# A 26-product second matmul in the last two token groups, and a spread transform tail

## The chip, the cores and the metric

The kernel runs on one core of a Trainium2 chip. A core has engines that work beside each other, each with its own queue of instructions: TensorE (PE) multiplies matrices, VectorE (DVE) and ScalarE (ACT) work on tiles in on-chip memory (SBUF) and in the matmul accumulators (PSUM), GpSimd (POOL) works on SBUF, and SyncE (SP) mostly starts transfers (DMAs). An instruction that waits holds up all that stand behind it in its own queue. The metric is the device time of one execution in microseconds (us). All data is fp32.

## The reference

Attention within chunks of 64 tokens, for 8 batches, 8 heads, 576 tokens and 64 channels a head, gives x of 8 x 576 x 512. Then comes a Fourier mix with a feed-forward block:

```python
attn = softmax(q_c @ k_c^T / sqrt(64)); x = attn @ v_c      # per chunk of 64 tokens
mixed = real(fft(fft(x, axis=1), axis=2))
u = x + mixed
un = (u - mean(u)) / sqrt(var(u) + 1e-6)                     # over 512 channels
ch = maximum(un @ w1, 0) @ w2                                # 512 x 2048, 2048 x 512
return u + ch
```

## The kernel before, in words

**Groups.** The 4608 token rows are cut into nine groups of four tiles of 128 rows. Groups 0 to 7 hold most of one batch each, in pairs of a lower and an upper tile; group 8 holds the four tiles that are left over from the middle chunks. The main loop runs `mlp(g)` for the nine groups: an "up" (un @ w1, relu) and a "down" (@ w2, added to u and stored). Each is a generator of steps, and t counts the steps over the whole kernel. `begin[g]` is the step at which group g begins; KF is 16, HF is 8.

**Products.** Group 0 multiplies plainly: `up_first`, and `down_plain` (16 steps of four matmuls dn, L1236; L1249 adds u). From group 1 on, `up_halves` and `down_halves` treat the matrices as 2x2 blocks and make 7 products where 8 would be plain. The up (L1289, accumulators pa and pb) goes through w1 in four pairs of 7 products; ACT and DVE put the accumulators together (L1294 to L1309). The down (L1341) makes 7 products of two rows of eight matmuls: 112 matmuls of 128x128 by 256. Its operand sums are made during the up by `operands` (L1167 and L1168 on DVE, L1169 on POOL), its output sums by DVE (L1350 to L1361) and POOL (L1353, L1354, L1373, L1378).

The down of the last group, `down_few` (L1405), cuts the matrices in 4x4 by 4x2 blocks and makes 26 products of four matmuls, 104 in all. The list `PRODUCTS` gives for each product its operand, its weight block, its accumulator, what DVE adds to the output after it (L1415), and the operand sums that POOL makes behind it (`sums`, L1183). Six operand sums (`EARLY`) are made during the up. `FEW` is the first group whose down is done in this way.

**Weights.** In group 0 the weights arrive and are rounded by DVE and ACT (`round_weight`, L362 to L386). POOL makes the sums of w1's blocks (`keep1`, four sums for each of four pairs, L1069) and of w2's (`keep2`, L1087). They are stored in DRAM (`keep1_store`, L1091; L1099 for w2) as slabs. Group 1's up still reads the parts of w1 where they were made; later groups fetch slabs, all on SP's queue: `fetch(1)` brings w1 slabs of 256 KB into a ring of ten (tile wa, L1155), `fetch(2)` w2 slabs of 1 MB into a ring of three (tile wb, L1160), `fetch(3)` the blocks for `down_few`, 512 KB each, into a ring of NS3 places (L1158): six in wb, the rest in tiles named more.

**make_rest.** Of the blocks that `down_few` multiplies by, 19 are sums. `make_rest` computes them on POOL in two halves of the columns: for each half it loads eight blocks of w2 (L1124, 256 KB each), makes 23 sums (`MADE`, L1133) and stores 19 of them (L1140). Buffers come from a list `spare` of 14 places that attention and transform no longer use; a buffer whose sum is stored comes free when the store has landed. It is a generator, advanced in the main loop from t = `ready_at[NG - 3]` on, two sums a step, and in the kernel before it ends during group 7's down.

**Attention and transform.** `side(b)` is the attention and transform of batch b, cut into `sizes[b - 1]` steps that are spread over the feed-forward steps before group b begins. In the main loop `due` is the number of side steps that must be done by step t, from `ready_at`. The end of the transform is a list of mixes (L838, three for an odd batch), each read by ACT (L843) and DVE (L848, L849), added to x (L855 on DVE and POOL), and normalised: `normed` writes un on ACT (L992), `turned` transposes it on PE (L397, pt) and copies it (unT, L1007), `combined` makes the three block sums of the up on DVE (L1024 to L1026). For group 1 the last three are called from `down_plain` of group 0 at given steps m. The attention uses the accumulator `att` of pool ps_a for its scores (sc, L448) and DVE transposes for q and k (L416); L418 copies one column of each transposed tile on POOL.

**Stores.** `store` writes a finished tile. A lower tile goes by POOL (L1037). An upper tile goes by four transfers of 64 KB, two from SP and two from ACT (L1046).

Queues are in program order; the tile framework adds the waits on data and on free buffers, and a rotation of eight lanes for SP's transfers, so that each waits for the one eight before it.

Of the kernel before, what the change touches and what calls it, by code (L numbers as in the profile page):

```python
# [16 lines left out]
def kernel(  # L17
# [36 lines left out]
    CH = 64  # L54
# [100 lines left out]
    NR2, NS3 = len(PRODUCTS), 11  # L155
# [245 lines left out]
    def att_T(n, which="qk"):  # L401
# [4 lines left out]
        if n > first[2]:  # L406
            for src, dst, nm in ((qs, qT, "qT"), (ks, kT, "kT")):
                if nm[0] not in which:
                    continue
                a = src.pop(n).rearrange("p j (t b d) -> p j t b d", t=4, b=2)[:, :, :, 0]  # L410
                t = one_p.tile([128, NJ, 2, CH + 1], FP32, tag=nm, name=nm)
                low = kind(n) == LO and nm == "qT"
                to = t[:, :, :, CH:0:-1] if low else t[:, :, :, 0:CH]
                if kind(n) == HI:
                    to = to[:, :, ::-1]
                nc.vector.transpose(out=to.rearrange("p j c (r t) -> p j t c r", t=4), in_=a)  # L416
                if low:
                    nc.gpsimd.tensor_copy(t[:, :, :, 0:1], t[:, :, :, CH:CH + 1])  # L418
                dst[n] = t.rearrange("p j c t -> p (j c) t")
            if n + 1 < NT:  # L420
                load(n + 1, which)
            return
# [369 lines left out]
    def fourier(b):  # L792
# [36 lines left out]
        def mixed(i):  # L829
            mix = ps_t.tile([128, 512], FP32, tag="pt", name="mix")  # L830
# [142 lines left out]
    uns, unTs = {}, {}  # L973
# [56 lines left out]
    def store(n, o):  # L1030

        last = n in groups[-1][1::2]
        for h, (b, c) in enumerate(chunks(n)):
# [37 lines left out]
    def keep1_store(i):  # L1071
        pair, o = i // NO, (2, 1, 5, 3, 0, 4, 6)[i % NO]
# [35 lines left out]
    def make_rest():  # L1108
# [6 lines left out]
        for tag, n in (("q", 2), ("k", 2), ("zf", 2), ("two", 1), ("qT", 1), ("kT", 1), ("pT", 1)):  # L1115
            t = one_p.tile([128, n * z], FP32, tag=tag, name="part")
            spare += [t[:, i * z:(i + 1) * z] for i in range(n)]
        last = {x: i for i, text in enumerate(MADE) for x in text.replace("=", "-").replace("+", "-").split("-")}
        for half in range(2):
            part = slice(half * z, (half + 1) * z)  # L1120
            where, behind = {}, []
            for name in ("b31", "b41", "b42", "b11", "b32", "d", "w", "b21"):
                where[name] = spare.pop(0)
                nc.sync.dma_start(out=where[name], in_=block_of(name)[:, part])  # L1124
                if half and name in ("b41", "b11", "d"):
                    yield
            yield
            for i, text in enumerate(MADE):
                name = text.split("=")[0]
# [99 lines left out]
    def down_plain(g, h1):  # L1229
# [4 lines left out]
        for m in range(KF):  # L1234
# [202 lines left out]
    with tc.manual_schedule():  # L1437
# [63 lines left out]
        ready_at = [begin[g] + (2 * KF - 7 if g < first_of[2] else 2 * HF + 4) for g in range(NG)]  # L1501
        conv2 = iter([step for i in range(HF // 2) for step in [keep2(i ^ 1)]])
# [8 lines left out]
        for g in range(NG):  # L1511
            for _ in mlp(g):
# [7 lines left out]
                if cur < len(sides):  # L1520
                    t0 = 3 if cur == 0 else ready_at[cur - 1]
                    t1 = ready_at[cur]
                    due = min(sizes[cur], (t - t0) * sizes[cur] // (t1 - t0))
                    while done < due:
# [20 lines left out]
                if begin[1] - 1 <= t < begin[1] + 7 and t % 2:  # L1545
# [71 lines left out]
```

## Time and profile before

| | us |
|---|---|
| median of 3 runs (1068.7 to 1071.26) | 1069.43 |
| profiled execution, whole time | 1068.75 |
| its span in the trace | 1067.0 |
| PE busy in the span | 1044.8 |
| up(1) of group 1 starts (first L1289) | 192.41 |
| group 7: up starts, down starts | 869.69, 918.04 |
| group 8: up starts, down starts | 968.14, 1016.49 |

The granted PE clock was 0.999 of full speed. A row of the timeline gives start, duration, engine, line, operation, the tiles (out<-in), and in brackets the idle time before it with what ended it. PE records each fp32 matmul as two, so `x8` is four matmuls.

### The profile page before, as it was taken

Reading aid. Unit: us, or ns where it says so; the run is one execution under the profiler, and the core shown is the slowest. Engines: PE = TensorE matmul, PEld = TensorE weight load, DVE = VectorE, ACT = ScalarE, POOL = GpSimd, SP = SyncE. Lnnn points to the kernel's source line nnn. Section 1 sums busy time; section 2 is a strip of 40 time slices with the busy share of each in tenths; the row PEclk is TensorE's granted clock in tenths of the full one; section 3 lists DMA queues with packets and bytes.
Section 4 is the critical chain, followed back from the end, with each engine's and each line's share of the span. In section 5 each row is a group of like instructions: output and inputs, shape, how many; then the busy total and the mean of one; then the engine's idle time right before and its main releaser. Section 6 shows DMA issues by size and latency. Waiting matters only on the chain.

```text
span 1067.0 us, 20226 instructions
## 1 busy us (share of the span) xinstructions
PE 1044.8 (98%) x7498; PEld 854.8 (80%) x7498; DVE 610.8 (57%) x1319; ACT 315.4 (30%) x746; POOL 429.6 (40%) x563
## 2 busy tenths in 40 slices
PE   8999989999999999999999999999999999999997
PEld 6645444788888888888888888888888888888886
DVE  4798986784567465664565555745564545333331
ACT  4688563233113411322022312331133103101200
POOL 4310018772425141344234321624261656680281
PEclk9999999999999999999999999999999999999999
DMA  8777565689568546873677359835753579677663
GB/s 174 216 208 215 126 197 182 179 260 341 169 201 232 148 150 201 240 222 118 193 210 222 109 172 254 241 111 173 212 162 120 204 220 350 205 232 234 239 231 105
DMA packets 164352, 212.81 MB, mean 199 GB/s; under 512 B 76924, under 2 KB 110716, under 8 KB 157982
## 3 DMA queue, kind: packets, MB, share of 16 engines
q1 hardware_dynamic: 151900, 203.85, 62.2%
q0 software_dynamic: 9024, 4.91, 2.2%
q10 hardware_dynamic: 3330, 2.76, 1.0%
q8 instruction: 60, 0.98, 0.4%
q14 instruction: 38, 0.31, 0.1%
HBM read 177.31 MB, written 34.08 MB: 198 GB/s over the span
## 4 chain that ended last, share of the span: by engine, by line
PE 84%; DVE 5%; ACT 4%; DMA 2%; SPq 2%; POOL 1%; issue 1%; ACTq 0%; DVEq 0%; POOLq 0%
PE pa L1289 21%; PE pb L1341 18%; PE pb L1289 16%; PE pa L1341 14%; PE dn L1405 4%; PE pt L397 3%; PE mix L838 2%; PE xp L498 2%; PE z L719 1%; PE sc L448 1%; SPq L263 1%; PE up L1195 1%; DVE power L378 1%; PE dn L1236 1%; DMA yall<-in_moe_w_ch_dram 1%
## 5 line engine op out<-in xcount | busy, mean ns | idle before, releaser
L1289 PE MATMUL pa<-unT,wa 128*128 128x256 f32 x736 | 174.9, 380 | 0.0
L1289 PEld LDWEIGHTS pa<-unT,wa 128*128 128x128 f32 x736 | 138.3, 190 | 19.1
L1289 PE MATMUL pb<-wa 128*128 128x256 f32 x448 | 106.6, 381 | 0.0
L1341 PE MATMUL pa<-wb,h 128*128 128x256 f32 x448 | 101.5, 380 | 0.0
L1341 PE MATMUL pb<-wb,h 128*128 128x256 f32 x448 | 100.7, 379 | 0.0
L1289 PEld LDWEIGHTS pb<-wa 128*128 128x128 f32 x448 | 84.3, 190 | 11.5
L1341 PEld LDWEIGHTS pa<-wb,h 128*128 128x128 f32 x448 | 83.9, 190 | 11.3
L1341 PEld LDWEIGHTS pb<-wb,h 128*128 128x128 f32 x448 | 84.1, 190 | 11.0
L1169 POOL TENSOR_TENSOR h<-h 128x256 f32<-128x256 f32 x56 | 47.9, 864 | 100.8 <-DVE wb L1167 97.1
L1037 POOL DMA_DIRECT2D out_dram<-wb x28 | 18.8, 674 | 118.0 <-DVE wb L1358 81.8
L1295 DVE TENSOR_TENSOR wa<-pb,wa 128x256 f32<-128x256 f32 x56 | 23.8, 425 | 70.2 <-ACT wa L1294 70.2
L1289 PE MATMUL pb<-unT,wa 128*128 128x256 f32 x256 | 60.5, 379 | 0.0
L1294 ACT COPY wa<-pa 128x256 f32<-128x256 f32 x56 | 20.8, 372 | 124.3 <-DMA out_dram<-wb 68.0
L1236 PE MATMUL dn<-wb,h 128*128 128x512 f32 x128 | 57.5, 597 | 0.0
L1303 ACT ACTIVATE h<-pa 128x256 f32<-128x256 f32 x64 | 24.5, 383 | 111.3 <-PE pa L1289 110.8
L1289 PE MATMUL pa<-wa 128*128 128x256 f32 x224 | 54.0, 384 | 0.0
L1289 PEld LDWEIGHTS pb<-unT,wa 128*128 128x128 f32 x256 | 48.6, 190 | 6.6
L1309 ACT ACTIVATE h<-h 128x512 f32<-128x512 f32 x64 | 39.8, 629 | 42.5 <-DVE h L1308 42.3
L1341 PE MATMUL pb<-wb,yall 128*128 128x256 f32 x224 | 51.2, 381 | 0.0
L1341 PE MATMUL pb<-wb 128*128 128x256 f32 x224 | 50.7, 379 | 0.0
L1341 PE MATMUL pa<-wb,yall 128*128 128x256 f32 x224 | 50.5, 379 | 0.0
L1195 PE MATMUL up<-unT,wa 128*128 128x512 f32 x108 | 49.4, 598 | 0.0
(301 smaller groups left out, 1996.8 us busy)
## 6 DMA issues: line engine op xcount, KB each, us to landing
wb<-s SPq DMA_DIRECT2D x49, 1024.0 KB, 5.4
wa<-s SPq DMA_DIRECT2D x196, 256.0 KB, 4.4
xall<-in_moe_w_ch_dram SPq DMA_DIRECT2D x22, 512.0 KB, 4.4
q<-in_q_dram SPq DMA_DIRECT2D x96, 112.0 KB, 3.7
k<-in_k_dram SPq DMA_DIRECT2D x96, 112.0 KB, 4.7
wb<-s SPq DMA_DIRECT2D x16, 512.0 KB, 5.1
v<-in_v_dram SPq DMA_DIRECT2D x124, 64.0 KB, 3.9
s<-part SPq DMA_DIRECT2D x30, 256.0 KB, 6.2
```

Of the source, the lines that this page charges most:

```text
L397: nc.tensor.transpose(pt[:, j, :], src(j), ident)
L498: nc.tensor.matmul(out=xp[0][e][t0:t0 + CH, j * DV:(j + 1) * DV], lhsT=a[r0:r0 + CH, j, t0:t0 + CH], rhs=b[r0:r0 + CH, c, j, :], start=Tru ...
L838: nc.tensor.matmul(out=mix[:, cols], lhsT=zt[:, T], rhs=tab, start=(T == 0), stop=(T == 3), skip_group_check=True,)
L1169: nc.gpsimd.tensor_tensor(out=h1[:, m, hi], in0=h1[:, m, lo], in1=h1[:, m, hi], op=ALU.subtract)
L1195: nc.tensor.matmul(out=up, lhsT=w1[:, kk, m * 128:(m + 1) * 128], rhs=unT[:, kk], start=(kk == 0), stop=(kk == KD - 1), skip_group_check=True,
L1236: nc.tensor.matmul(out=dn, lhsT=h1[:, m, s * 128:(s + 1) * 128], rhs=w2[:, m, :], start=(m == 0), stop=(m == KF - 1),)
L1289: nc.tensor.matmul(out=dst, lhsT=w[:, kk, r], rhs=rhs[o][:, kk], start=(o in (0, 1) and kk == 0), stop=(kk == 1), skip_group_check=True,)
L1295: nc.vector.tensor_tensor(out=b, in0=pbs[r][:, 0], in1=a, op=ALU.add)
L1303: nc.scalar.activation(out=h1[:, m, lo], in_=dst, func=ACTF.Relu)
L1309: nc.scalar.activation(out=h1[:, HF + m], in_=h1[:, HF + m], func=ACTF.Relu)
L1341: nc.tensor.matmul(out=dst, lhsT=lhs[:, m], rhs=w[:, m], start=(o in (0, 2) and m == 0), stop=(m == HF - 1), skip_group_check=True,)
L1405: nc.tensor.matmul(out=dst, lhsT=lhs[:, m], rhs=w[:, m], start=(fresh and not half and m == 0), stop=(m == 3), skip_group_check=True,)
```

## The change

- `FEW` becomes NG - 2, so that groups 7 and 8 both use `down_few`. Group 7's `operands` sums, output sums on POOL and w2 slabs are gone; 26 more operand sums (L1183) and 26 more fetches of 512 KB come in. `make_rest` now ends within group 7's up: it has 21 spare buffers, starts with 13 loads, and loads the rest as buffers come free. NS3 goes from 11 to 8; the two places outside wb are tiles of the tags q and k, which `make_rest` used as buffers.
- For group 1 the side's end moves two steps later (`ready_at[0]`, `late_due`); the third mix gets the accumulator `att`; `normed` and `turned` have other steps; `combined` is called from the main loop behind the side's step (`joined`).
- `keep1(0)` comes between the second and third part of `keep2`; the stores of w1's parts are in another order, at other steps.
- Upper tiles' stores all go from SP. The column copies of the first batches' tiles (n < first[3]) go from POOL to VectorE.

```diff
-    NR2, NS3 = len(PRODUCTS), 11
+    NR2, NS3 = len(PRODUCTS), 8
...
-                    nc.gpsimd.tensor_copy(t[:, :, :, 0:1], t[:, :, :, CH:CH + 1])
+                    eng = nc.vector if n < first[3] else nc.gpsimd
+                    eng.tensor_copy(t[:, :, :, 0:1], t[:, :, :, CH:CH + 1])
...
-            mix = ps_t.tile([128, 512], FP32, tag="pt", name="mix")
+            if (b, i) == (1, NM - 1):
+                mix = ps_a.tile([128, 2, 512], FP32, tag="att", name="mix")[:, 0]
+            else:
+                mix = ps_t.tile([128, 512], FP32, tag="pt", name="mix")
...
-                    eng = nc.scalar if r else nc.sync
-                    eng.dma_start(out=out[b, t0 + 1 - r:t0 + CH:2, :], in_=o[r0 + ODD * r:r0 + ODD * r + ODD])
+                    nc.sync.dma_start(out=out[b, t0 + 1 - r:t0 + CH:2, :], in_=o[r0 + ODD * r:r0 + ODD * r + ODD])
...
-        for tag, n in (("q", 2), ("k", 2), ("zf", 2), ("two", 1), ("qT", 1), ("kT", 1), ("pT", 1)):
-            t = one_p.tile([128, n * z], FP32, tag=tag, name="part")
+        for pool, tag, n in (
+            (one_p, "q", 2), (one_p, "k", 2), (one_p, "zf", 2), (one_p, "two", 1), (one_p, "qT", 1), (one_p, "kT", 1),
+            (one_p, "pT", 1), (two_p, "ex", 1), (two_p, "ex", 1), (two_p, "pm", 1), (two_p, "pm", 1),
+            (three_p, "y", 1), (three_p, "y", 1), (three_p, "y", 1),
+        ):
+            t = pool.tile([128, n * z], FP32, tag=tag, name="part")
...
+        def take(keep):
+            while wanted and len(spare) > keep:
+                half, name = wanted.pop(0)
+                places[half][name] = spare.pop(0)
+                nc.sync.dma_start(out=places[half][name], in_=block_of(name)[:, half * z:(half + 1) * z])
+
+        take(8)
+        yield
...
+                take(7)
                 if i % 2:
                     yield
 
-    FEW = NG - 1
+    FEW = NG - 2
...
             for j in range(G):
-                due = KF - (G - j + 1)
-                if m == due - 2:
+                if m == (10, 10, 12, 12)[j]:
                     normed(g + 1, j)
-                if m == due:
+                if m == (12, 13, 14, 14)[j]:
                     turned(g + 1, j)
                     if j >= 2 and g + 1 >= first_of[1]:
-                        combined(g + 1, j - 2)
+                        joined.append((g + 1, j - 2))
...
-        ready_at = [begin[g] + (2 * KF - 7 if g < first_of[2] else 2 * HF + 4) for g in range(NG)]
-        conv2 = iter([step for i in range(HF // 2) for step in [keep2(i ^ 1)]])
+        ready_at = [begin[g] + (2 * KF - 5 if g < first_of[2] else 2 * HF + 4) for g in range(NG)]
+        late_due = {ready_at[0] - 4 + i: sizes[0] - x for i, x in enumerate((3, 3, 2, 1, 0))}
+
+        def first_sums():
+            keep1(0)
+            yield
+
+        conv2 = iter([keep2(1), keep2(0), first_sums(), keep2(3), keep2(2)])
...
+                while joined:
+                    combined(*joined.pop(0))
...
-                if t == ready_at[NG - 3]:
+                if t == ready_at[FEW - 1]:
                     rest_ = make_rest()
-                    next(rest_)
-                if t > ready_at[NG - 3] + 4 and (t < begin[NG - 2] or t % 4 != 3):
+                if t >= ready_at[FEW - 1] and (t >= begin[FEW] or t % 4 != 3):
                     next(rest_, None)
-                if t == begin[FEW] + 2:
-                    more = [xall[:, 2 * G:2 * G + 4, :].rearrange("p a f -> p (a f)")[:, i * Z3:(i + 1) * Z3] for i in range(2)]
-                    more += [one_p.tile([128, Z3], FP32, tag=tag, name="more") for tag in ("q", "k", "zf")]
-                    slab3.extend(a.rearrange("p (m e) -> p m e", m=4) for a in more)
-                if begin[FEW] + 2 <= t < begin[FEW] + 2 + NS3:
+                if t == begin[FEW] + 2 * HF - 1:
+                    for _ in rest_:
+                        pass
+                    slab3.extend(
+                        one_p.tile([128, Z3], FP32, tag=tag, name="more").rearrange("p (m e) -> p m e", m=4)
+                        for tag in ("q", "k")
+                    )
+                if begin[FEW] + 2 * HF - 4 <= t < begin[FEW] + 2 * HF:
                     fetch(3)
-                if begin[1] < t < begin[1] + KF:
-                    for i in range(2):
-                        if n_kept < HF // 2 * NO:
-                            keep1_store(n_kept)
-                            n_kept += 1
+                    fetch(3)
+                if KF < t <= KF + 4 or KF + 8 <= t < KF + 16:
+                    keep1_store(n_kept // 3, (0, 4, 6)[n_kept % 3])
+                    n_kept += 1
+                if begin[1] <= t < begin[1] + KF:
+                    keep1_store((t - begin[1]) // 4, (2, 1, 3, 5)[(t - begin[1]) % 4])
```

More of the change, by code (lines that the diff above doesn't have):

```diff
@@ L970, in fourier_early @@
         yield
-    uns, unTs = {}, {}
+    uns, unTs, joined = {}, {}, []
     def natural(n):
@@ L1069, in keep1, with keep1_store @@
             nc.gpsimd.tensor_tensor(out=out_, in0=in0, in1=in1, op=op)
-    def keep1_store(i):
-        pair, o = i // NO, (2, 1, 5, 3, 0, 4, 6)[i % NO]
+    def keep1_store(pair, o):
         to = s1[pair, o].rearrange("p (k x) -> p k x", k=2)
@@ L1114, in make_rest @@
             spare.append(xall[:, 2 * G:2 * G + 4, :].rearrange("p a f -> p (a f)")[:, i * z:(i + 1) * z])
-        for tag, n in (("q", 2), ("k", 2), ("zf", 2), ("two", 1), ("qT", 1), ("kT", 1), ("pT", 1)):
-            t = one_p.tile([128, n * z], FP32, tag=tag, name="part")
+        for pool, tag, n in (
[4 more added lines that the diff above has]
+            t = pool.tile([128, n * z], FP32, tag=tag, name="part")
             spare += [t[:, i * z:(i + 1) * z] for i in range(n)]
         last = {x: i for i, text in enumerate(MADE) for x in text.replace("=", "-").replace("+", "-").split("-")}
-        for half in range(2):
[L1120 to L1127, printed above, removed]
+        places = [{}, {}]
+        wanted = [(half, name) for half in range(2) for name in ("b31", "b41", "b42", "b11", "b32", "d", "w", "b21")]
+        def take(keep):
[5 more added lines that the diff above has]
+        yield
+        for half in range(2):
+            part, where, behind = slice(half * z, (half + 1) * z), places[half], []
             for i, text in enumerate(MADE):
-                name = text.split("=")[0]
                 to = spare.pop(0)
@@ L1523 @@
                     due = min(sizes[cur], (t - t0) * sizes[cur] // (t1 - t0))
+                    if cur == 0:
+                        due = late_due.get(t, (t - t0) * sizes[cur] // (t1 - 2 - t0))
                     while done < due:
@@ L1544 @@
                         pass
-                if begin[1] - 1 <= t < begin[1] + 7 and t % 2:
+                if begin[1] < t < begin[1] + 7 and t % 2:
                     keep1((t - begin[1] + 1) // 2)
-                if t == ready_at[NG - 3]:
+                if t == ready_at[FEW - 1]:
                     rest_ = make_rest()
-                    next(rest_)
-                if t > ready_at[NG - 3] + 4 and (t < begin[NG - 2] or t % 4 != 3):
+                if t >= ready_at[FEW - 1] and (t >= begin[FEW] or t % 4 != 3):
                     next(rest_, None)
-                if t == begin[FEW] + 2:
-                    more = [xall[:, 2 * G:2 * G + 4, :].rearrange("p a f -> p (a f)")[:, i * Z3:(i + 1) * Z3] for i in range(2)]
-                    more += [one_p.tile([128, Z3], FP32, tag=tag, name="more") for tag in ("q", "k", "zf")]
-                    slab3.extend(a.rearrange("p (m e) -> p m e", m=4) for a in more)
-                if begin[FEW] + 2 <= t < begin[FEW] + 2 + NS3:
-                    fetch(3)
-                if begin[1] < t < begin[1] + KF:
-                    for i in range(2):
-                        if n_kept < HF // 2 * NO:
-                            keep1_store(n_kept)
-                            n_kept += 1
+                if t == begin[FEW] + 2 * HF - 1:
[6 more added lines that the diff above has]
+                if begin[FEW] + 2 * HF - 4 <= t < begin[FEW] + 2 * HF:
+                    fetch(3)
+                    fetch(3)
[4 more added lines that the diff above has]
+                    keep1_store((t - begin[1]) // 4, (2, 1, 3, 5)[(t - begin[1]) % 4])
                 if t in (begin[1] + 9, begin[1] + 13, begin[1] + 16):
```

## The prediction

> **What bounds the kernel now.** I read the page first, its busy times and its chain of waits; then the idle time of TensorE (PE) in the timeline around the passage from group 0 to group 1; then the chain's pieces from 860 us on, the windows by stretch of the same time, and GpSimd's (POOL's) timeline there. From the page:
>
> ```profile
> span 1067.0 us, 20226 instructions
> PE 1044.8 (98%) x7498; PEld 854.8 (80%) x7498; DVE 610.8 (57%) x1319; ACT 315.4 (30%) x746; POOL 429.6 (40%) x563
> PE 84%; DVE 5%; ACT 4%; DMA 2%; SPq 2%; POOL 1%; issue 1%; ACTq 0%; DVEq 0%; POOLq 0%
> ```
>
> PE is the bound. A matmul less is its pitch less; work elsewhere counts only where PE stands idle for it. PE's timeline in the passage, the rows with idle time in brackets:
>
> ```profile
> 150.01 0.49 PE L838 MATMUL mix<-ce,zr 128*128 128x129 f32 x2 [1.67 <-ACT zr L785]
> 157.97 0.46 PE L838 MATMUL mix<-ce,zf 128*128 128x129 f32 x2 [2.06 <-DVE y L849]
> 171.84 0.66 PE L397 MATMUL pt<-ident,un 128*128 128x128 f32 x4 [1.41 <-ACT un L992]
> 181.36 0.62 PE L498 MATMUL xp<-v,pT 64*64 64x65 f32 x26 [0.41 <-ACT unT L1007]
> 192.41 1.99 PE L1289 MATMUL pb<-xall,wb 128*128 128x256 f32 x8 [2.40 <-POOL wb L1069]
> ```
>
> They sum to 7.95 us. After 222 us PE has no gap over 0.1 us until its last matmul; the chain there is PE alone:
>
> ```profile
> 1014.76 1.73 PE pa L1289 x8
> 1016.49 44.91 PE dn L1405 x208
> ```
>
> One step of 1.73 us is one product, four matmuls in eight records. L1405 x208 is the 26-product down of group 8, 1.727 us a product. DMA and POOL in group 7's up and down, the windows (PE, PEld, DVE, ACT, POOL busy, granted clock, DMA share, GB/s), then POOL's rows:
>
> ```profile
> 870.00:880.00 10.00, 10.00 (x48) 8.81 (x47) 3.18 (x8) 1.82 (x5) 5.96 (x5) 1.00 0.97 313
> 880.00:890.00 10.00, 10.00 (x48) 8.81 (x47) 5.08 (x11) 2.91 (x7) 7.95 (x7) 1.00 1.03 369
> 890.00:900.00 10.00, 10.00 (x48) 8.79 (x48) 5.54 (x13) 3.00 (x7) 6.62 (x6) 1.00 0.97 352
> 900.00:910.00 10.00, 10.00 (x48) 8.81 (x47) 4.71 (x12) 3.61 (x8) 4.31 (x4) 1.00 0.97 341
> 910.00:918.00 8.00, 8.00 (x39) 7.04 (x38) 4.87 (x12) 2.29 (x5) 4.64 (x5) 1.00 0.68 233
> ```
>
> ```profile
> 874.85 1.27 POOL L1133 TENSOR_TENSOR part<-xall 128x512 f32<-128x512 f32 x1 [3.88 <-DMA out_dram<-wb]
> 884.59 2.50 POOL L1133 TENSOR_TENSOR part<-part 128x512 f32<-128x512 f32 x2 [1.88 <-DMA s<-part]
> ```
>
> The 16 DMA engines are already full from 870 to 910 us, moving 313 to 369 GB/s: 0.84 to 0.71 us for a block of 256 KB. A POOL sum takes 1.27 us. 15.6 MB moved from 870 to 918.
>
> **Part 1: group 7's down with 26 products.** 104 matmuls take the place of 112: 8 x 0.432 us = 3.45 us less on PE (1.727 / 4 each). No doubt about this term. With it go, in group 7, the operand sums L1167 to L1169 (16 on VectorE, 8 on POOL at 0.86) and the output sums L1373, L1378, L1353 and L1354 on POOL: all lay beside PE, worth nothing, and POOL's time is spent on 26 block sums instead.
>
> What it adds: make_rest, 46 sums on POOL (58 us at 1.27), and 38 stores of 256 KB with 16 loads. It starts where it started, but must be done when group 7's down starts (918.04 us in the old clock) instead of by group 8's; the last sums and stores are where this is tight.
>
> POOL first. By 869.7 some 12 of the 46 sums are done; 34 are left, and six early operand sums of group 7: 40 x 1.27 = 50.8 us without a wait, to 920.5. The down's first products read blocks that need none of these; the block sums between products then follow, with the closest two, for products 5 and 9, some 4 to 5 us ahead of PE if POOL starts them at 918. So POOL may be 2.5 + 1.6 us behind, and 1.6 us of waits cost nothing. In the old rows above POOL waited 3.88 + 1.88 us in this stretch, for buffers still being stored; the change has 21 spare buffers for 14. Bounds 0 to 5 us of PE time; I take 0, because a stall by the next item covers it.
>
> DMA second. The fetch of product 6's slab (s19) goes into a tile of tag q, which is one of make_rest's own buffers, and so waits until the store of s12, second-last of all, has landed. In SP's new order there lie ahead of that fetch, from the store of s15 in the second half on: 17 stores and 12 loads of w1 of 256 KB, and six slabs of 512 KB: 41 blocks. That store is issued when the eighth sum of the second half is done: 869.7 + 19 x 1.27 = 893.8, with some 2 us of waits 896. 41 blocks at 0.71 to 0.84 take 29.1 to 34.4 us: 925.1 to 930.4. [...] PE wants it at 918.04 + 6 x 1.727 = 928.4. [...] I take 4.5. Outer bounds: 0 (the queue runs faster than its rows) and 12 (sums late as well). Later slabs need 512 KB in 1.727 us, 304 GB/s, below every full row: no further stall.
>
> [...]
>
> **Part 2: the tail of group 1's transform.** The first mix moves behind 4 more down matmuls (3.45 us), so its 1.67 us gap goes. The third gets 4 ahead of it and its own PSUM bank, so the 2.06 for L849 goes; the un gap of 1.41 and the 0.41 go in the same way, with the turns one step later or spread. keep1(0), four POOL sums whose second-to-last start made the 2.40, moves ahead of eight others and would end near 178 us. All five: -7.95.
>
> New waits: the scores use the bank that the third mix now has, and on ScalarE the two L992 (0.81 each) stand ahead of its copy: about 1.4 us. The last two turns now come together, 5.0 us ahead of up(1) (pt 0.44, dn 3.44, xp 0.63, sc 0.47), and both combinations (L1024 to L1026) must be made on VectorE in that time. Their duration depends on POOL:
>
> ```profile
> 182.00 1.38 DVE L1025 TENSOR_TENSOR xall<-unT,xall 128x256 f32<-128x256 f32 x1
> 187.69 0.43 DVE L1025 TENSOR_TENSOR xall<-unT,xall 128x256 f32<-128x256 f32 x1
> ```
>
> At 182 POOL was summing back to back (3.45 us for the three), at 187.69 it stood idle (1.2). With eight L1087 sums now there, the slow row is the nearer: the second L1025 ends 0.1 + 3.45 + 2.0 = 5.6 us after the last turn, 0.6 late. A later turn of ex, 0.4. Net -7.95 + 1.4 + 0.6 + 0.4 = -5.6. Bounds: -8.3 (no new wait, and part of the 0.20 and 0.57 us at 218 and 222 gone) and -2.5 (L1025's delay and the scores' both twice over, 0.6 + 1.4 more, with 1 for loads of k now behind L1091's stores on SP).
>
> The stores of w1's parts move to other steps on SP; up(1) reads the parts in place, and slabs of them are fetched only after its sixteenth step, with the down of group 1 to cover the last store: nothing. The next keep1, due four POOL sums after the outputs of group 0, keeps 2 to 3 us.
>
> **Part 3: copies and upper stores.** Two or three copies of 0.226 us go from POOL to VectorE, 57% busy: nothing, at most 0.2 each in the tail. Upper stores: four on SP instead of two on SP and two on ScalarE. SP waits for L1024 there (27.1 us in six waits), and two more issues of some 0.5 us wait behind it, with the w1 loads behind them; the ring of ten slabs hides that. Bounds 0 to 1, taken 0.
>
> **Sum.** -3.45 - 5.6 + 4.5 + 0 = -4.55. The profiled execution took 1068.75 (span 1067.0): 1064.2. The median shown is 1069.43, 0.68 above; with that 1064.9, and 1064.5 between the two. 0.3% (3.2 us) is about what a measurement of this kernel tells from no change: 1066.2 to 1072.6.
>
> **Rivals.** *No stall at group 7's down.* DMA showed bursts above its mean, and the engines drop to share 0.68 at 910, so there is room; against it, that room is what the added stores and the seven earlier slabs fill. 1069.43 - 3.45 - 5.6 = 1060.4.
>
> *Slower: POOL and DMA both fall behind in group 7.* The place is the start of its down. Full DMA delays the landing that frees buffers, POOL waits for buffers, its stores come late, and the slabs with them. It decides from a stall of 12.3 us on (3.45 + 5.6 + 3.2). By POOL alone that takes 13.9 us of waits, more than twice the 5.8 shown, and more spare buffers speak against it; that the up of group 7 has no slack left on either speaks for it. At 14 us: 1074.
>
> *The tail gives its gain back.* ScalarE's order or VectorE under POOL's sums makes new waits of 6 us in place of 8: -3.45 - 2 + 4.5, 1068.5. The contended rows speak for it, but four more matmuls of cover per step against it.
>
> *Only stores and copies matter, to nothing:* not possible for the product count, which is fixed by the code.
>
> **How the numbers follow.** Likeliest 0.50, own range 1061.5 to 1067.5; no stall 0.22; tail lost 0.15; slower 0.13. Faster: 0.43 of the likeliest, 0.22, and 0.02 of the tail's: 0.67. Same: 0.07 + 0.12 = 0.19. Slower 0.14. The range, 1058.5 to 1071, takes in the no-stall case with the tail's best, and the tail's loss; beyond it lie the slower rival and little else.
>
> **What would show it.** 7,482 matmul records, 16 fewer. up(1) starts near 187 instead of 192.4, with a gap before the scores. In group 7 a PE gap of some 4.5 us before the seventh product, its releaser a DMA into a tile named more; POOL's sums back to back up to the start of that down. Wrong: no such gap, or one before an earlier product (POOL the releaser), or gaps in up(1) after its start.

## The result and the profile after

The changed kernel takes 1079.74 us (median of 4, 1078.72 to 1081.26) where the kernel before took 1069.30 beside it: a ratio of 1.0091, 95% interval 1.0074 to 1.0108. It is 10 us slower; the prediction was 1064.5, with 1071.0 as its upper end. The profiled execution took 1081.26 us.

The page of the kernel after, its span, busy times and chain:

```profile
span 1079.4 us, 20225 instructions
PE 1049.5 (97%) x7482; PEld 856.4 (79%) x7482; DVE 605.7 (56%) x1323; ACT 315.6 (29%) x744; POOL 446.5 (41%) x571
PE 81%; DVE 5%; DMA 5%; SPq 3%; ACT 3%; issue 1%; POOL 0%; ACTq 0%; DVEq 0%; POOLq 0%
```

The 16 records are gone, and yet PE is busy for 4.7 us more. That is the first thing to explain. 8 matmuls fewer should have given 1044.8 - 3.45 = 1041.35; PE was busy for 1049.5, so 8.15 us went into matmuls that ran slower in this execution. The gaps over 0.1 us sum to 24.0 us, where they were 16.4. So of the 12.4 us of span all but 0.1 are -3.45 for the products, +8.15 for slow matmuls and +7.6 for gaps.

PE's timeline in the passage, rows with a gap and one behind (start, duration, and in brackets the idle time before):

```profile
170.83 0.66 PE L397 MATMUL pt<-ident,un 128*128 128x128 f32 x4 [1.71 <-ACT un L996]
173.46 1.14 PE L449 MATMUL sc<-kT,qT 64*64 64x64 f32 x32 [1.98 <-DVE y L853]
174.53 5.75 PE L1246 MATMUL dn<-wb,h 128*128 128x512 f32 x8
192.51 3.57 PE L1298 MATMUL pb<-xall,wb 128*128 128x256 f32 x8 [2.06 <-DVE o L1259]
215.79 3.31 PE L1298 MATMUL pb<-unT,wa 128*128 128x256 f32 x8 [2.00 <-DVE xall L1304]
```

The two mix gaps and the xp gap are gone, as predicted; the gap for un is not (1.71 us, 1.41 before), and up(1) starts at 192.51 and not at 187. And the matmuls behind three of the gaps take 1.6 to 1.8 times as long as before: 5.75 us for 3.60, 3.57 for 1.99, 3.31 for 1.89. In the windows the granted clock is 0.69 and 0.63 from 170 to 180 us, 0.74 from 190, 0.66 from 215. In the kernel before, gaps of 2.06 and 2.40 us left it at 1.00; the last section shows what tells the two cases apart.

Group 7's down, PE's rows up to the eighth product:

```profile
921.92 3.62 PE L1414 MATMUL dn<-wb,h 128*128 128x256 f32 x16
926.51 3.69 PE L1414 MATMUL dn<-wb,yall 128*128 128x256 f32 x16 [0.97 <-DMA wb<-s]
932.85 3.57 PE L1414 MATMUL dn<-wb,yall 128*128 128x256 f32 x8 [2.65 <-DMA wb<-s]
936.21 2.02 PE L1414 MATMUL dn<-wb,h 128*128 128x256 f32 x8
942.54 5.38 PE L1414 MATMUL dn<-more,h 128*128 128x256 f32 x16 [4.31 <-DMA more<-s]
```

The windows of the same time (PE, PEld, DVE, ACT, POOL, granted clock, DMA share, GB/s):

```profile
870.00:880.00 10.00, 10.00 (x48) 8.80 (x47) 4.37 (x10) 0.74 (x2) 8.57 (x8) 1.00 0.60 171
910.00:920.00 10.00, 10.00 (x48) 8.79 (x48) 3.40 (x8) 2.06 (x7) 9.84 (x9) 1.00 0.94 262
930.00:940.00 10.00, 5.58 (x17) 4.10 (x16) 2.26 (x6) 0.00 (x0) 9.04 (x8) 0.83 0.95 357
940.00:950.00 10.00, 7.46 (x27) 6.31 (x28) 1.62 (x4) 0.00 (x0) 3.15 (x4) 0.83 1.00 374
```

And SP's queue there (L1149 a store of make_rest, L1168 a fetch for `down_few`, some rows left out):

```profile
915.54 1.80 SPq L1149 DMA_DIRECT2D s<-part  x2
922.66 0.79 SPq L1168 DMA_DIRECT2D wb<-s  x2
...
932.78 1.55 SPq L1149 DMA_DIRECT2D s<-part  x2
938.52 0.80 SPq L1168 DMA_DIRECT2D more<-s  x2
```

Product 6 starts 942.54 - 921.92 = 20.62 us after the down's start; 6 x 1.727 = 10.36 was wanted. It is 10.26 late, and the smaller gaps before it and their slow matmuls lie inside that. The two products behind it take 5.38 for 3.62: 1.76 more. 10.26 + 1.76 - 3.45 = 8.57, which is what group 7's down lost against the kernel before. Up to the start of that down the loss is 4.0 us: 0.3 were lost ahead of 145 us, 3.7 in the passage and in up(1).

### The profile page after: what moved, and what is told of

Its sections match the earlier page's. It is cut to its first block, busy times and chain, and to the rows that moved or that the text cites. A ratio compares the mean times of both kernels' runs of the same rounds, so it can differ in the third digit from the quotient of the medians.

```text
span 1079.4 us, 20225 instructions
## 1 busy us (share of the span) xinstructions
PE 1049.5 (97%) x7482; PEld 856.4 (79%) x7482; DVE 605.7 (56%) x1323; ACT 315.6 (29%) x744; POOL 446.5 (41%) x571
## 4 chain that ended last, share of the span: by engine, by line
PE 81%; DVE 5%; DMA 5%; SPq 3%; ACT 3%; issue 1%; POOL 0%; ACTq 0%; DVEq 0%; POOLq 0%
PE pa L1298 20%; PE pb L1350 15%; PE pb L1298 15%; PE pa L1350 12%; PE dn L1414 8%; PE pt L397 2%; DMA xall<-in_moe_w_ch_dram 2%; PE mix L842 2%; SPq L263 2%; PE xp L499 1%; PE z L720 1%; PE sc L449 1%; PE up L1205 1%; DMA out_dram<-o 1%; PE dn L1246 1%
## 5 line engine op out<-in xcount | busy, mean ns | idle before, releaser
L1350 PE MATMUL pa<-wb,h 128*128 128x256 f32 x384 | 87.2, 380 | 0.0
L1350 PE MATMUL pb<-wb,h 128*128 128x256 f32 x384 | 86.4, 379 | 0.0
L1179 POOL TENSOR_TENSOR h<-h 128x256 f32<-128x256 f32 x48 | 40.8, 859 | 102.6 <-DVE wb L1177 100.2
L1350 PEld LDWEIGHTS pa<-wb,h 128*128 128x128 f32 x384 | 71.8, 190 | 9.7
L1350 PEld LDWEIGHTS pb<-wb,h 128*128 128x128 f32 x384 | 72.0, 190 | 9.4
L1193 POOL TENSOR_TENSOR h<-h 128x512 f32<-128x512 f32 x36 | 45.1, 1270 | 25.4 <-ACT h L1318 16.5
L1414 PE MATMUL dn<-wb,h 128*128 128x256 f32 x224 | 50.6, 380 | 0.0
L481 ACT COPY pT<-pt 128x512 f32<-128x512 f32 x36 | 21.0, 582 | 101.0 <-PE pt L397 100.7
```

Of the source, the lines that this page charges most:

```text
L1179: nc.gpsimd.tensor_tensor(out=h1[:, m, hi], in0=h1[:, m, lo], in1=h1[:, m, hi], op=ALU.subtract)
L1193: nc.gpsimd.tensor_tensor(out=out_, in0=a, in1=b, op=op)
L1350: nc.tensor.matmul(out=dst, lhsT=lhs[:, m], rhs=w[:, m], start=(o in (0, 2) and m == 0), stop=(m == HF - 1), skip_group_check=True,)
L1414: nc.tensor.matmul(out=dst, lhsT=lhs[:, m], rhs=w[:, m], start=(fresh and not half and m == 0), stop=(m == 3), skip_group_check=True,)
```

## The experiments

Each ratio is to the kernel before, run beside it; 0.001 is 1.07 us. Ratios are compared, since the median of the kernel before lay between 1069.3 and 1071.9 from one set of runs to another. Line numbers are each kernel's own.

**The parts one by one.** e1 has the products alone (FEW, `make_rest`, NS3 and its fetches), e2 the tail and w1's order alone, e4 stores and copies alone, e3 everything but the upper stores:

```diff
-                    nc.sync.dma_start(out=out[b, t0 + 1 - r:t0 + CH:2, :], in_=o[r0 + ODD * r:r0 + ODD * r + ODD])
+                    eng = nc.scalar if r else nc.sync
+                    eng.dma_start(out=out[b, t0 + 1 - r:t0 + CH:2, :], in_=o[r0 + ODD * r:r0 + ODD * r + ODD])
```

> The kernel before with the products of group 7 alone (FEW, make_rest, slabs, NS3); copies, upper stores and the transform's tail as before. Theory A: the loss in group 7 belongs to this part, landings of stores ahead of the slabs and the slow PE clock after each gap: in the profile of the changed kernel group 7's down cost 8.6 us more than before, so 1069.3 + 8.6 = 1077.9. Theory B: the upper stores on SP crowd SP's queue in group 7, and without them the stall is the 4.5 us of the prediction: 1069.3 - 3.45 + 4.5 = 1070.4.

> The kernel before with the spread tail of group 1's transform and the new order of w1's sums and stores alone. Theory A: up(1) starts where it did (0.1 us later in the profile of the changed kernel), with the slow clock after its gap 1.7 us more, and the late loads of q (gap of 2.00 us at 215.79) belong to the upper stores on SP, so they are absent: about 1070.5. Theory B: the late loads belong to the stores of w1's parts on SP, in this part: about 1073.5. The prediction's term for this part: 1063.7.

> The changed kernel with the second half of the upper stores back on ScalarE. Theory A: the eight upper stores stood on SP from 194.4 to 204.0 us and held back the loads of v and q; with four there the gap of 2.00 us at 215.79 and the 1.4 us of slow clock behind it go: 1079.7 - 3.4 = 1076.3. Theory B (w1's parts' stores hold the loads): 1079.7.

> The kernel before with the upper stores all on SP and the column copies of the first tiles on VectorE, nothing else. Theory A: loads of q for up(1) come late behind eight stores, a new gap of up to 2 us and slow clock behind it: 1070.5 to 1073. Theory B, and the prediction's term: nothing, 1069.3.

| | ratio, 95% | us |
|---|---|---|
| e1, products | 1.0086 (1.0060 to 1.0113) | +9.2 |
| e2, tail | 1.0001 (0.9989 to 1.0013) | +0.1 |
| e4, stores and copies | 1.0017 (1.0001 to 1.0032) | +1.8 |
| e3, the change less upper stores | 1.0089 (1.0058 to 1.0119) | +9.5 |

The three parts sum to 11.1 us, the whole change measured 9.7: they add up within their intervals. The loss is the products'; the tail brings nothing; e3 refutes the theory that the upper stores make q and k late in up(1): its gap of 2.01 us at 215.64 is still there.

e4 points to a cost that was thought to be none; its interval begins close to 1, and the copies were not run without the stores. In the kernel before, the copy L418 on POOL waited for VectorE and so held keep1(0) back while VectorE made its block sums:

```profile
189.60 0.20 POOL L418 COPY qT<-qT 128x8 f32<-128x8 f32 x1 [3.69 <-DVE qT L416]
```

With the copy gone, POOL's sums run beside them. VectorE's rows in e4 (kernel before: 0.42, 0.43 and 0.42 for the second set of three):

```profile
190.14 1.35 DVE L1025 TENSOR_TENSOR xall<-unT 128x256 f32<-128x256 f32 x1
191.52 1.37 DVE L1026 TENSOR_TENSOR xall<-unT,xall 128x256 f32<-128x256 f32 x1
192.82 1.48 DVE L1027 TENSOR_TENSOR unT<-unT 128x256 f32<-128x256 f32 x1
```

Behind these three stand the evictions of group 0's accumulators, and up(1) starts with a gap of 3.34 us in place of 2.40, its first product at 3.38 us.

**Group 7: transfers, queue, or clock.** f1 fetches no w1 slabs for group 8, f2 puts matmuls of zeros in PE's gaps, f3 issues `make_rest`'s stores from ScalarE.

```diff
-        if which == 1 and i < HF // 2 * NO * (NG - 2):
+        if which == 1 and i < HF // 2 * NO * (NG - 3):
...
+            if g == FEW and o in (2, 4, 6):
+                fill = ps_a.tile([128, 2, 512], FP32, tag="att", name="fill")[:, 0, 0:256]
+                for _ in range({2: 2, 4: 5, 6: 9}[o]):
+                    nc.tensor.matmul(out=fill, lhsT=warm[:, 0:128], rhs=warm[:, 0:256], start=True, stop=True)
...
-                    nc.sync.dma_start(out=block_of(old)[:, part], in_=where[old])
+                    nc.scalar.dma_start(out=block_of(old)[:, part], in_=where[old])
```

> The changed kernel without the 28 loads of w1 slabs for group 8 (its up multiplies by the slabs left over from group 7, so group 8's rows are wrong). Theory A: group 7's slabs come late because transfers and SP's queue are full; 7.3 MB less and no waits for PE between the stores: the three gaps (7.93 us) and the slow clock behind them (4.1 us) nearly go, some 10 us under the changed kernel, 1069 to 1071. Theory B: POOL's sums end too late whatever the transfers do (the last at 926.96 us, 5 us after the down's start): at most 2 us under the changed kernel.

> The changed kernel with 2, 5 and 9 matmuls of zeros into an accumulator that nobody reads, ahead of products 2, 4 and 6 of group 7, where PE has its gaps. Theory A: the slow PE clock behind a gap comes from the idle time itself; with PE busy the clock stays at 1.00 and the 4.1 us go: 4 us under the changed kernel. Theory B: the clock follows something else (power, transfers): the same as the changed kernel or longer.

> The changed kernel with make_rest's 38 stores issued from ScalarE. Theory A: SP's order is what delays them, since on SP they stand behind w1 loads that wait for PE's products; the last store then leaves right after the last sum (927 us in place of 934), product 6's slab comes some 5 us sooner: 4 to 8 us under the changed kernel with its clock. Theory B: the transfers are full in any case and the order does not matter: within 2 us of it.

f1: 1.0045 (1.0029 to 1.0060), 4.9 us under the changed kernel; group 7's down cost 5.7 us in its profile. Between the two theories: the transfers matter, but product 6 still came 17.0 us after the start, with the DMA share down to 0.64 from 910 to 920. f2: 1.0069 (1.0043 to 1.0095), and its time decides nothing: product 6's slab came 22.0 us after the start, so that filling the gaps before it could gain nothing; they lie under that wait in any case. But product 4, behind a gap of 0.71 in place of 2.65, took 1.97 us in place of 3.57, and products 6 and 7, behind a gap of 2.96 that the fill had left, still took 5.38: with PE kept busy the clock stayed. f3: 1.0057 (1.0036 to 1.0078). Product 6 starts 16.5 us after the down's start, so the queue's order matters too, but ScalarE now waits for POOL's sums, and the up loses most of what the down gains:

```profile
888.29 3.30 PE L1298 MATMUL pa<-wa 128*128 128x256 f32 x8 [2.07 <-ACT wa L1303]
```

**The two holes in SP's queue.** In SP's rows above SP stood still from 917.3 to 922.7, with s8's fetch at its head waiting for s8's own store to land, and from 934.3 to 938.5 waiting for s12's. g1 takes the two places named more from the tags k and zf; g2 puts the fetches for products 2 to 7 behind all stores; g3 does both.

```diff
-                        for tag in ("q", "k")
+                        for tag in ("k", "zf")
...
-                if begin[FEW] + 2 * HF - 4 <= t < begin[FEW] + 2 * HF:
-                    fetch(3)
-                    fetch(3)
+                if t == begin[FEW] + 2 * HF - 4:
+                    fetch(3)
+                    fetch(3)
+                if t == begin[FEW] + 2 * HF - 1:
+                    for _ in range(6):
+                        fetch(3)
```

> The changed kernel with the two places named more taken from the tags k and zf in place of q and k. Theory A: product 6's slab waits for the landing of s12's store, the last but one, because that store reads from q; on k no such wait is left, and SP does not stand still from 934.3 to 938.5 us: s19 lands 4 us sooner, 4 us under the changed kernel. Theory B: what makes it late is the full transfers ahead of it, and another place changes nothing: within 1.5 us.

> The changed kernel with the fetches for products 2 to 7 behind all of make_rest's stores in SP's order, where products 2 to 5 stood between them. Theory A: the fetch of s8 stood at SP's head for 5.3 us (917.3 to 922.7) until its own store had landed, and held back the stores behind it; without that hole the last store leaves when POOL's last sum is done (927 us) in place of 934, and s19 lands some 4 us sooner, though s8 comes later: 2 to 4 us under the changed kernel. Theory B: POOL's end and full transfers decide, and s8 is now late itself: 0 to 4 us over it.

> Both: the fetches for products 2 to 7 behind the stores, and the places from k and zf. Theory A, both holes in SP's queue gone: 5 to 8 us under the changed kernel, 1072 to 1075. Theory B, transfers and POOL decide: within 2 us of the changed kernel.

Both single edits measured 1.0062 (1.0041 to 1.0083), 3.1 us under the changed kernel; g3 1.0047 (1.0032 to 1.0062), 4.7 under. So the holes are real; g2 gained what was expected, g1 and g3 a little less. The intervals of g1 and g2 still overlap the changed kernel's, g3's does not. In g1 SP issued s19's fetch at 931.85, 13.3 us after the down's start and not 16.6, and the slab still came 20.0 after it: the fetch took 6.6 us where it had taken 4.0. In g3 one gap is left, ahead of product 2.

**POOL's end, and the slow clock.** h2 is g3 with the six EARLY sums of group 7 on VectorE; h4 is g3 with 16 matmuls of zeros ahead of product 2.

```diff
-                    sums(h1, EARLY.split()[turn_ - 1:turn_])
+                    sums(h1, EARLY.split()[turn_ - 1:turn_], nc.vector if g == FEW else nc.gpsimd)
```

> As g3_both, with the six early operand sums of group 7 on VectorE in place of POOL. Theory A: POOL's last sum sets the last store and with it s8's fetch; 7.6 us less on POOL bring it some 4 to 7 us forward, and the one gap of 7.48 us shrinks to 1 to 4: 3 to 7 us under g3_both. Theory B: transfers are full and POOL's end does not matter: within 1.5 us of g3_both.

> As g3_both, with 16 matmuls of zeros (6.9 us) into an accumulator that nobody reads, ahead of product 2 of group 7, in the gap of 7.48 us. Theory A: the slow clock of the four products behind the gap (0.67 from 930 to 935 us, 1.9 us lost) follows from PE's idle time and goes: the products run at 1.727 us from the first on, 1.9 us under g3_both. Theory B: it follows from something else and stays: the same as g3_both.

h2: 1.0053 (1.0035 to 1.0070), the same as g3. POOL's last block sum of g3, then of h2:

```profile
923.02 1.26 POOL L1142 TENSOR_TENSOR part<-part,xall 128x512 f32<-128x512 f32 x1
```

```profile
918.87 1.28 POOL L1142 TENSOR_TENSOR part<-part,xall 128x512 f32<-128x512 f32 x1
```

It ends 5.4 us after the down's start in g3 and 0.2 after it in h2, and product 2 starts 11.1 us after it in both. PE in g3, then PE and the windows of h2:

```profile
929.92 7.07 PE L1414 MATMUL dn<-wb,yall 128*128 128x256 f32 x24 [7.48 <-DMA wb<-s]
```

```profile
931.09 7.62 PE L1414 MATMUL dn<-wb,yall 128*128 128x256 f32 x24 [7.53 <-DMA wb<-s]
...
920.00:925.00 5.00, 3.56 (x17) 2.80 (x15) 1.27 (x3) 0.65 (x2) 4.23 (x5) 1.00 1.05 405
925.00:930.00 5.00, 0.00 (x0) 0.00 (x0) 0.00 (x0) 0.00 (x0) 3.37 (x3) 0.87 1.06 353
```

So with the holes closed POOL does not decide: the DMA engines are full (1.05, 1.06) up to the moment PE goes on, and SP's last store left 4 us after the sum was made. What is late, then, is the volume of stores, w1 loads and slabs. f1's gain points the same way, but no run takes out the holes and the w1 loads together.

h4: 1.0046 (1.0030 to 1.0061), the same as g3. The fill ended at 928.8 and left a gap of 2.30 us, and the clock fell behind that as it had behind 7.48:

```profile
925.00:930.00 5.00, 3.83 (x18) 3.04 (x16) 0.00 (x0) 0.00 (x0) 4.84 (x5) 1.00 1.02 370
930.00:935.00 5.00, 3.87 (x10) 3.18 (x11) 0.42 (x1) 0.00 (x0) 1.61 (x2) 0.66 1.03 419
```

The three products behind it took 7.10 us (g3: 7.07; at full clock 5.35). So a gap of 2.30 us cost as much slow time here as one of 7.48. That idle time causes it is not settled by this run, since the fill was too short; the profiles of all runs together bear on it (last section).

**The passage: POOL beside VectorE.** t1 leaves out POOL's sums of keep2(3) and keep2(2); f4 puts w1's stores back where they were.

```diff
-            nc.gpsimd.tensor_tensor(out=out_, in0=in0, in1=in1, op=op)
+            if i < 2:
+                nc.gpsimd.tensor_tensor(out=out_, in0=in0, in1=in1, op=op)
             yield
```

> The changed kernel without POOL's eight sums of keep2(3) and keep2(2), which run from 180 to 191 us beside VectorE's block sums of group 1 (their stores stay, so parts of w2's sums are wrong). Theory A: VectorE's rows beside them are stretched (1.50 us for 0.42), which makes the evictions of group 0's last accumulators late (gap of 2.06 us at 192.51) and SP waits for these sums ahead of the loads of q and k (2.00 at 215.79): both gaps and the slow clock behind them go, 4 to 7 us under the changed kernel. Theory B: VectorE's own order sets the eviction, and the transfers the loads: within 1.5 us.

> The changed kernel with the stores of w1's parts in the order and at the steps of the kernel before. Theory A: those stores, spread between the loads on SP, are what makes q and k late in up(1); without them the gap of 2.00 us at 215.79 and the 1.4 us of slow clock go: 3.4 us under the changed kernel. Theory B: the loads stand behind the s2 stores and the outputs of group 0: the same as the changed kernel, within 1.5 us.

t1: 1.0025 (1.0014 to 1.0036), 7.1 us under the changed kernel. VectorE's block sums in the changed kernel, then in t1, with PE's start of up(1):

```profile
185.25 1.50 DVE L1028 TENSOR_TENSOR xall<-unT 128x256 f32<-128x256 f32 x1 [5.16 <-ACT unT L1011]
189.48 1.49 DVE L1028 TENSOR_TENSOR xall<-unT 128x256 f32<-128x256 f32 x1
191.00 0.42 DVE L1029 TENSOR_TENSOR xall<-unT,xall 128x256 f32<-128x256 f32 x1
```

```profile
185.15 0.42 DVE L1028 TENSOR_TENSOR xall<-unT 128x256 f32<-128x256 f32 x1 [4.35 <-ACT unT L1011]
186.28 0.42 DVE L1028 TENSOR_TENSOR xall<-unT 128x256 f32<-128x256 f32 x1
...
190.28 1.99 PE L1299 MATMUL pb<-xall,wb 128*128 128x256 f32 x8
```

POOL's sums ended at 190.7 in the changed kernel, and from then on the rows of VectorE are short. Without the sums up(1) starts without a gap and has none up to group 1's down, which starts 3.4 us sooner than in the kernel before. The expected 4 to 7 us are there. t1 leaves work out, so this is what those sums cost beside VectorE and ahead of the loads, both together, and not a gain to be had. f4: 1.0092 (1.0065 to 1.0118), the same as the changed kernel. In its profile, the fastest of its four executions, the gap of 2.00 is gone, but one of 1.40 stands in group 1's down, for a slab of w2, and group 7's down loses 9.6 us: the place of w1's stores moves the waits and gains nothing.

**All work done, sums moved.** Three kernels move half of those sums past up(1)'s start: h1 (on e2) keep2(3), i1 (on e2 with stores and copies as changed) keep2(2), i2 as i1 with keep2(2)'s four stores issued from POOL. h3 is h1 with the products of h2. The edit of i1, against the changed kernel's tail:

```diff
-        conv2 = iter([keep2(1), keep2(0), first_sums(), keep2(3), keep2(2)])
+        conv2 = iter([keep2(1), keep2(0), first_sums(), keep2(3)])
...
+                    if t == begin[1] + 1:
+                        for _ in keep2(2):
+                            pass
                     keep1((t - begin[1] + 1) // 2)
```

> The kernel before with the spread tail of group 1's transform (as in e2_tail), and keep2(3), four sums and four stores, moved behind keep1(1), past the start of up(1). Theory A: POOL's sums beside VectorE's block sums of group 1 are what eats the tail's gain; half of them gone from that place, the evictions come in time and q and k load sooner: 3 to 5 us under e2_tail and the kernel before, 1066 to 1069 where before is 1071.5. Theory B: the four sums are then missing for keep1(2) and up(1) waits for POOL: the same as before or longer.

> Products of group 7 as in h2_early_dve, tail as in h1_keep2_later, copies and upper stores as before. If both theories A hold: before - 3.45 for the products, 1 to 4 for the gap left, - 3 to 5 for the tail: 1 to 6 us under the kernel before. If the theories B hold: 4 us over it.

> The kernel before with the spread tail, the upper stores on SP and the copies on VectorE (all of the change but the products of group 7), and keep2(2), four sums, behind the start of up(1), ahead of keep1(1). Theory A: with half of POOL's sums gone from beside the block sums of group 1 up(1) starts 2 to 3 us sooner than in the kernel before and without a slow clock, and keep1(1) ends near 201 us, just in time for the second pair: 2 to 4 us under the kernel before. Theory B: keep1(1), 5 us later, holds up(1): no gain, up to 4 us over it.

> As i1_keep2_2_later, with the four stores of keep2(2) issued by POOL behind keep1(1). Theory A: q and k come in time, the gaps of 1.27 and 2.52 us and the slow clock behind them go: 3 to 6 us under i1_keep2_2_later, 2 to 4 us under the kernel before. Theory B: the loads are late because of full transfers or their place behind the outputs of group 0: within 1.5 us of i1_keep2_2_later.

h1: 1.0041 (1.0027 to 1.0055). up(1) starts at 189.01, 3.4 us sooner than before, and then loses more to two waits that the move made: VectorE's L515 writes the part of xall that the moved sums' stores still read, and four upper stores fill ScalarE's queue ahead of L1295:

```profile
210.46 0.76 DVE L515 TENSOR_TENSOR xall<-xp,rd 128x256 f32<-128x256 f32 x2 [6.68 <-DMA s<-xall]
...
188.11 6.42 ACTq L1049 DMA_DIRECT2D out_dram<-o  x4
```

i1: 1.0010 (0.9997 to 1.0022). No gap at up(1)'s start, but q and k come late (gaps of 1.27 and 2.52). i2: 0.9986 (0.9972 to 1.0000), 1.5 us under the kernel before; of the 3 to 6 us that were expected over i1 it brought 2.6, and not in the way expected: two gaps (1.18 and 2.75) are still there, as long together as i1's. What its profile lacks is slow clock, 3.4 us of it where i1's has 10.2. So the theory on the moved stores is not confirmed. i2 is the fastest of all these kernels, and its interval touches 1. h3, with the products, measured 1.0103 (1.0085 to 1.0121): neither half had a gain, and what the two lose adds up.

## Why the prediction was wrong

*Part 1, products: predicted +1.05 (-3.45 + 4.5), measured alone +9.2.* The -3.45 was right, and so was the place: product 6, its slab behind the landing of the second-last store; the smaller gaps ahead of products 2 and 4 were not foreseen. What failed is the walk of SP's queue to that landing. "41 blocks at 0.71 to 0.84" gave 29.1 to 34.4 us; in the changed kernel 39.5 went by from s15's store at 898.99 us to s19's fetch at 938.52, with two blocks more. It began within 1 us of where it was put, counted from the down's start, and the fetch took 4.0. So s19 landed 20.6 us after the down's start, where PE wanted it 10.36 us after that start, and "I take 4.5" stood in for what measured 10.26. The walk had no holes. It left out that a fetch of a block just stored stands at SP's head until the store has landed, 5.3 us for s8, with too little in flight behind it (262 GB/s from 910 to 920). The 4.5 also has in it the author's estimate of how long s12's store takes to complete, which no run shows; SP stood still for that store for 4.2 us, and it landed 5.7 us after its issue. The holes are not all of it: with both closed (g3) 4.7 us come back, and group 7's down still loses 5.9 in the profile. There the transfers are the limit, as predicted; h2 rules out POOL's end, which was 5.0 us behind the down's start in the changed kernel where 2.5 was said. The rows of 405 and 419 GB/s in h2 and h4 lie above the 313 to 369 of the rows that the prediction called full, so those were no ceiling here.

*Part 2, the tail: predicted -5.6, measured alone +0.1.* "Net -7.95 + 1.4 + 0.6 + 0.4" is where it failed. The gaps of the mixes, of xp and of POOL's keep1 went as said; that of un did not (1.71, where 1.41 was to go), the scores waited 1.98 (1.4 taken), and VectorE's rows were the slow ones, as chosen. But 0.6 priced only the wait for the operands. Behind the two stretched combinations stand the four evictions that free up(1)'s accumulator: a gap of 2.06 in the whole change and 2.49 in e2. The loads of q and k behind L1091's stores (those of w2's sums; `keep1_store` is L1074), which stood only in the bound with 1 us, were a gap of 2.00 (3.08 in e2). In t1 both are gone: POOL's sums cause both, and the share of each is not shown.

*Part 3: predicted 0, measured +1.8 (1.0001 to 1.0032).* In e4's profile the copy's wait on POOL had been what kept POOL and VectorE apart. "Nothing" was the wrong term, if the stores have no part in it; the cover named, VectorE at 57%, was an average.

*The term that was in no sum:* slow matmuls, 8.15 us in the profile. Without them the change would have cost some 4.3 us of span. The prediction, its bounds and all rivals took a gap at its own length, and in the kernel before, with gaps of 2.06 and 2.40 at a granted clock of 1.00, that was so.

Of the rivals, *the tail gives its gain back* (0.15) had the tail's mechanism, VectorE under POOL's sums. The slower one (0.13) had the place, the start of group 7's down, but not the road: it wanted a stall of 12.3 us, from POOL waiting for buffers, and POOL waited for them for 2.9 us in that stretch. What came was 10.3 of stall, 1.8 of slow clock and a tail that brought nothing.

## What to carry to other kernels

Walk a transfer queue with its waits, not by bytes alone: a fetch issued right behind the store that it reads holds up everything after it, here for 5.3 us (s8). Where an instruction waits between two engines that share work on the same memory, its wait may be what keeps them out of each other's way (with it gone, the second set of three rows of VectorE took 1.35 to 1.48 us each in e4, where they had taken 0.42); ask what runs side by side when it goes. And price a gap on TensorE with the slow stretch that can follow it, 1.4 to 1.8 us for each one of 3.4 us here, not with its length alone.

## What the runs showed of the hardware

**The clock.** In the changed kernel's profile the granted clock of PE is 1.00 except for five stretches at 0.50 (and the time behind the last matmul): from 171.87 us for 6.8, and from 192.35, 216.25, 933.05 and 943.29 for 3.4 each. These starts lie 6, 7, 210 and 3 times 3.413 us apart: all changes of the clock in this profile lie on one grid of that step. PE's busy time in a stretch of that grid and in the one behind it (start:end, length, PE busy, granted clock, DMA share, GB/s), for the gaps of 2.06 and 2.00 of the changed kernel, then for those of 2.06 and 2.40 of the kernel before, whose grid is laid by the same step from the fall of its clock at 1064.5:

```profile
188.94:192.35 3.41, 1.51 (x65) 1.00 1.01 348
192.35:195.77 3.42, 3.26 (x8) 0.50 0.81 230
212.83:216.25 3.42, 1.42 (x7) 1.00 0.83 259
216.25:219.66 3.41, 3.41 (x31) 0.50 0.67 196
```

```profile
156.54:159.95 3.41, 1.98 (x10) 1.00 0.00 0
159.95:163.37 3.42, 3.42 (x9) 1.00 0.27 96
190.68:194.09 3.41, 1.68 (x8) 1.00 0.43 120
194.09:197.51 3.42, 3.42 (x20) 1.00 0.57 146
```

Up to the last matmul, the five stretches ahead of a fall of the clock in the changed kernel had PE busy for 0.22 to 0.44 of them; every other one at full clock had 0.52 or more. In the kernel before the emptiest had 0.49, and the clock stayed at 1.00. In the profiles of all runs but e1's, whose mean clock was 0.944, all 45 stretches at full clock with PE busy for less than 0.42 of them were followed by one at half clock, and none with 0.48 or more was; between the two five were and four were not. A slow stretch was followed by a fast one where PE was busy for 0.84 of it or more, and by another slow one at 0.80 or less (in the changed kernel 0.95 or more, and 0.53). So in these profiles the clock went with PE's idle share within a stretch, and the same gap cost it or not by where the grid fell: a gap of 2.06 us did in the changed kernel, whose grid, counted back, begins 1.20 us into the span, and did not in the kernel before, where it begins at 2.95.

The clock went with the spread of one kernel's times: of twenty executions of the kernel before beside h1, those with a mean clock of 0.999 took 1068.8 to 1069.7 us, those at 0.994 to 0.996 took 1070.5 to 1074.5. In e4's profile 2.9 us were lost within the first 20 us, where the change does nothing: to a late load of k (a gap of 1.46 us) and a granted clock of 0.68 from 15 to 20 us (1.00 in the kernel before).

**POOL beside VectorE.** A VectorE row of 128x256 with two operands in SBUF took 0.42 us with POOL idle (kernel before, 187.23 to 188.45), and up to 1.50 while POOL ran 128x512 sums (changed kernel, from 185.25). In the changed kernel each such row ended 0.28 us behind the sum that was running when it began: rows begun at 185.25, 186.78, 188.07 and 189.48 ended at 186.75, 188.15, 189.55 and 190.97, and POOL's sums at 186.47, 187.87, 189.27 and 190.69.
